# Attention and two expert layers on one core: where v_m w_in and the scores stand in TensorE's queue

## The chip, the cores and the metric

One core of a Trainium2 chip runs the whole program in one launch. The metric is the device time of an execution in microseconds (us); of several executions the median is taken.

## The reference, cut to what matters

```python
a = softmax(phi, axis=seq)                   # b=8, h=8, s=576, m=32
k_m = einsum('bhsm,bhsd->bhmd', a, k)        # d=64
v_m = einsum('bhsm,bhsd->bhmd', a, v)
attn = softmax(q @ k_m.T / 8)                # 576 x 32 for each head: P
x = (attn @ v_m) as [4608, 512]
h = x @ w_in;  g = h - tanh(h);  x2 = g @ w_out          # d_ff = 2048
h = x2 @ w_in2; g = h if h > 0 else exp(h) - 1; out = g @ w_out2
```

The weights and all matrices are float32. The kernel splits what it multiplies with into a high and a low part (the helper `convert` does it for weights, 128 rows by 512 at a time) and adds three products.

## The kernel before, in words

**Stage 1** is `moe_kernel`'s loop over 64 `blocks`. A block is one slice of 288 tokens (`n`, two slices to a batch) with two of the eight pages of 256 hidden columns (`sw` is the pair of pages). Attention times w_in is not made in that order: `make_vw` first multiplies v_m with the two pages of w_in (L337, called v_m w_in below), two blocks share the result, and `h_unit` (L355, the P product) multiplies P with it. A block has two halves, one for each page, and a half is written out by hand in this order: the P product into `h_ps`; ScalarE's first functions of it (L366 to L368); a first `x_unit` (L406, the product with w_out, of an older slice); a round of the weight conversions; a first round of the attention units, `units.round()`; in the first half of an odd block v_m w_in for the next two blocks (L808; in block 1 page by page, one in each half); a second `x_unit`; VectorE's three operations on `h_ps` (L382 to L384); a second round of the units. Below, 7.0 is the first half of block 7.

**Attention** runs beside it as 16 units, two to a batch, each a Python generator (`Attention.unit`). A round takes every live unit one step, to its next `yield`, the oldest first. Unit `u` starts in a listed round (L634). The steps of a unit from 2 on, in rounds after its start: 1 a transpose (mT), 3 the largest value (bmax), 7 the sums k_m and v_m (km, 24 products), 9, 10, 12 and 13 transposes of q (pq), 11 that of k_m and v_m (kT_ps, after which v_m is there), 14 the scores (sc), 19 the split of P, 21 its store to DRAM. Between 3 and 4 and between 7 and 8 (`spaced`) a bank of PSUM is kept over the `yield`. Before the blocks, rounds are run until unit 1 has stored its P (L635); from the seventh on, each of them also takes a round of the conversions (`cv`).

**PSUM.** x, v_m w_in (two banks), the scores (two banks) and every other product of the units share the three banks of `misc`; the P product has four banks of its own and the conversions have one.

**Conversions.** `cv` is a queue: every second round starts one conversion of half a page, those in `first` ahead of those in `todo`. A conversion takes four operations of VectorE (L50, L51, L54, L57) and one of ScalarE (L48); all but those of the first layer's w_in take another of ScalarE (L62) and one of GpSimd (L64). The half pages of w_out pages 0 and 1 stand in `todo`; at block 0 pages 2 and 3 of w_in and w_out go into `first` (L770). `need` runs rounds of `cv` until a page is there, in block 1 with rounds of the units beside them (L560). When the last unit has stored its P, page 7 of w_out goes into `first` (L775); at blocks 26 and 30 pages 4 to 7 of w_in go in ahead of what is there.

Each engine takes its instructions in the order in which this Python code issues them; so does the DMA queue of SyncE, on which all loads and stores go. The order of the rounds therefore is the order of TensorE's, VectorE's and ScalarE's queues.

Stage 2 (layer 2, L466 and L508) begins at about 880 us and is not touched.

## Time and profile before

| | |
|---|---|
| median of 3 runs | 1699.24 us |
| lowest and highest | 1696.74 and 1699.35 us |
| the profiled execution, its own time | 1696.12 us |
| span of its trace, first to last instruction | 1694.1 us |
| mean granted TensorE clock | 0.975 of full speed |

The span is 2.0 us shorter than the time of the same execution; the rest lies around it. The profile lists, for each engine, when it was busy, and for each idle stretch what released the engine. PE is TensorE, PEld its weight loads, DVE VectorE, ACT ScalarE, POOL GpSimd.

### The profile page before, as it was taken

How to read it: one execution, taken by the hardware profiler on the slowest of the kernel's cores; microseconds unless marked ns; L12 is line 12 of the kernel's file. 1: busy time of each engine (PE TensorE's matmuls, PEld its weight loads, DVE VectorE, ACT ScalarE, POOL GpSimd, SP SyncE). 2: the span in 40 equal slices, each digit the busy share in tenths (PEclk: the TensorE clock that was granted, in tenths of full speed). 3: DMA queues.
4: the chain of work that ended last, by engine and by line, in shares of the span. 5: the costliest groups of instructions: out<-in, count | busy, mean ns of one | idle time of the engine just before them, and what ended most of it. 6: DMA issues, size and time to landing. Idle time of an engine off the chain costs nothing.

```text
span 1694.1 us, 28080 instructions
## 1 busy us (share of the span) xinstructions
PE 1589.7 (94%) x10742; PEld 1382.9 (82%) x10742; DVE 1146.7 (68%) x1680; ACT 896.6 (53%) x1623; POOL 745.2 (44%) x526
## 2 busy tenths in 40 slices
PE   6639899889999989999999999999999999999998
PEld 4528788778889989999999988888888888888886
DVE  6766667878888878888675655655565555565554
ACT  2436767767787768888763333333333333333332
POOL 1325556666675557777662322232232232232222
PEclk9769999999999999999999999999999999999999
DMA  9635766668565446666579321212121212121100
GB/s 235 191 117 160 203 192 207 206 203 251 191 229 175 163 149 217 214 221 206 169 254 351 105 63 50 64 49 74 39 75 50 63 50 75 50 70 55 29 9 25
DMA packets 142214, 232.90 MB, mean 137 GB/s; under 512 B 8704, under 2 KB 102912, under 8 KB 140032
## 3 DMA queue, kind: packets, MB, share of 16 engines
q1 hardware_dynamic: 142080, 231.11, 42.8%
q8 instruction: 84, 1.38, 0.3%
q14 instruction: 50, 0.41, 0.1%
HBM read 157.68 MB, written 73.40 MB: 136 GB/s over the span
## 4 chain that ended last, share of the span: by engine, by line
PE 60%; POOL 5%; DVE 4%; ACT 3%; issue 3%; DMA 1%; POOLq 0%; ACTq 0%; DVEq 0%
PE h_ps L466 24%; PE o_ps L508 23%; PE x_ps L406 9%; PE h_ps L355 4%; POOL g L391 2%; POOL v L373 2%; DVE s L383 1%; POOL wst L64 1%; DVE s L384 1%; DVE h_ps L382 1%; DMA x_dram<-x 1%; ACT t L366 1%; ACT x L412 1%; ACT big L377 1%; ACT g L390 0%
## 5 line engine op out<-in xcount | busy, mean ns | idle before, releaser
L406 PE MATMUL x_ps<-g,w 128*128 128x288 f32 x3072 | 448.6, 298 | 45.8 <-ACT w L62 25.8
L406 PEld LDWEIGHTS x_ps<-g,w 128*128 128x128 f32 x3072 | 420.3, 190 | 64.0 <-ACT w L62 26.3
L492 POOL TENSOR_TENSOR e<-hm,e 128x512 fp32r<-128x512 f32 x144 | 186.7, 1297 | 573.0 <-ACT e L491 525.6
L466 PE MATMUL h_ps<-x,wi 128*128 128x512 f32 (+1 forms) x1920 | 422.2, 370 | 0.0
L508 PE MATMUL o_ps<-wo,e 128*128 128x512 f32 x1728 | 420.3, 392 | 0.7 <-POOL e L492 0.7
L466 PEld LDWEIGHTS h_ps<-x,wi 128*128 128x128 f32 x1920 | 336.0, 188 | 65.7
L508 PEld LDWEIGHTS o_ps<-wo,e 128*128 128x128 f32 x1728 | 323.6, 188 | 72.4 <-POOL e L492 1.1
L477 ACT ACTIVATE t_ps<-hm 128x512 f32<-128x512 f32 x144 | 86.7, 602 | 500.7 <-DVE hm L476 500.7
L373 POOL TENSOR_TENSOR v<-t,u 128x576 f32<-128x576 f32 x128 | 183.9, 1437 | 183.5 <-ACT u L367 157.5
L391 POOL TENSOR_TENSOR g<-s,g 128x576 fp32r<-128x576 f32 x128 | 201.5, 1574 | 90.0 <-ACT g L390 86.0
L483 DVE SCALAR_TENSOR_TENSOR hm<-hm,t_ps 128x512 f32<-128x512 f32 x144 | 98.9, 687 | 200.3 <-ACT hm L478 200.3
L355 PE MATMUL h_ps<-p,vw 128*128 128x288 f32 x1536 | 233.4, 302 | 0.0
L355 PEld LDWEIGHTS h_ps<-p,vw 128*128 128x128 f32 x1536 | 214.8, 192 | 2.9 <-issue 2.4
L476 DVE TENSOR_SCALAR hm<-h_ps 128x512 f32<-128x512 f32 x144 | 99.5, 691 | 125.9 <-PE h_ps L466 123.2
L366 ACT ACTIVATE t<-h_ps 128x576 f32<-128x576 f32 x128 | 83.3, 650 | 131.0 <-PE h_ps L355 56.5
L383 DVE SCALAR_TENSOR_TENSOR s<-s,v 128x576 f32<-128x576 f32 x128 | 137.5, 1074 | 12.5 <-POOL v L373 12.5
L368 ACT ACTIVATE s<-u,bias 128x576 f32<-128x576 f32 x128 | 99.5, 777 | 33.2 <-POOL g L391 25.4
L384 DVE COPY_PREDICATED s<-big,h_ps 128x576 f32<-128x576 uint32 x128 | 106.7, 834 | 11.0
L382 DVE TENSOR_TENSOR h_ps<-h_ps,t 128x576 f32<-128x576 f32 x128 | 96.7, 755 | 13.4 <-ACT u L367 13.4
L485 DVE TENSOR_TENSOR hm<-hm,h_ps 128x512 f32<-128x512 f32 x144 | 98.9, 687 | 5.0
L484 DVE SCALAR_TENSOR_TENSOR hm<-hm,t_ps 128x512 f32<-128x512 f32 x144 | 98.9, 687 | 5.0
L377 ACT ACTIVATE big<-u,bias 128x576 f32<-128x576 f32 x128 | 98.0, 766 | 1.1 <-DVE s L384 0.9
(88 smaller groups left out, 1552.4 us busy)
## 6 DMA issues: line engine op xcount, KB each, us to landing
x_dram<-x SPq DMA_DIRECT2D x128, 288.0 KB, 3.0
xr<-x_dram SPq DMA_DIRECT2D x72, 512.0 KB, 3.8
p<-p_dram SPq DMA_DIRECT2D x62, 576.0 KB, 5.0
raw<-in_moe_w_in_dram SPq DMA_DIRECT2D x32, 512.0 KB, 4.5
raw<-in_moe_w_out_dram SPq DMA_DIRECT2D x32, 512.0 KB, 4.0
w_dram<-wst SPq DMA_DIRECT2D x32, 512.0 KB, 3.6
kv<-in_k_dram SPq DMA_DIRECT2D x16, 576.0 KB, 6.0
kv<-in_v_dram SPq DMA_DIRECT2D x16, 576.0 KB, 7.9
```

The source lines that it names most:

```text
L355: nc.tensor.matmul(ps[:, j, :NB], lhsT=vw[a][:, kc, c0 + 128 * j:c0 + 128 * j + 128], rhs=p[:, kc, b, :], start=(k == 0), stop=(k == 5))
L366: nc.scalar.activation(t, w[0], ACTF.Tanh)
L373: nc.gpsimd.tensor_tensor(v, t, u, op=ALU.mult)
L377: self.nc.scalar.activation(big, u, ACTF.Relu, bias=self.const["bias"][:, 1:2])
L382: nc.vector.tensor_tensor(d, d, t, op=ALU.subtract)
L383: nc.vector.scalar_tensor_tensor(s, s, G_B, v, op0=ALU.add, op1=ALU.mult)
L384: nc.vector.copy_predicated(s, big.bitcast(U32), d)
L391: nc.gpsimd.tensor_tensor(g[:, 1], s, r32(g[:, 0]), op=ALU.subtract)
L406: nc.tensor.matmul(ps, lhsT=wo[pg][a][:, j, 128 * dm:128 * dm + 128], rhs=self.g[n, pg][:, b, j, :], start=(k == 0), stop=(k == 11))
L466: nc.tensor.matmul(out, lhsT=w3[:, a, kc, 128 * j:128 * j + 128], rhs=x[:, b, kc, :], start=(i == 0), stop=(i == 11))
L492: nc.gpsimd.tensor_tensor(e[:, 1], hm, r32(e[:, 0]), op=ALU.subtract)
L508: nc.tensor.matmul(acc, lhsT=e[:, a, jj, 128 * tg:128 * tg + 128], rhs=w4[:, b, j, :], start=(k == 0 and jj == 0 and i == 0), stop=(k == l ...
```

## The change

Three things change. (1) v_m w_in of both pages (from block 3 on) is issued at the start of the second half of an odd block, ahead of its P product, if no unit keeps a bank over a `yield` just then (`held`); otherwise it is issued in the middle of the second half. (2) The scores of units 5 to 15 wait, step by step, until the round is one that a P product follows (the second of a half) and no bank is kept. A flag `busy` lets only one unit at a time be between its first transpose of q and its scores. (3) Every unit has one more empty step ahead of its scores.

```diff
--- before.py
+++ after.py
@@ -89,6 +89,7 @@
         self.q_p = pool("at_q", 2)
         self.phi_p = pool("at_phi", 2 if side == "left" else 1)
         self.loaded = {}
+        self.before_x, self.held, self.busy = False, 0, False
         fix = pool("at_fix", 1)
         self.n_t = 3 if side == "left" else 2
         self.kv = fix.tile([96, self.n_t, 4, 6, D], F32, name="kv")
@@ -151,7 +152,9 @@
         bmax = busy_tile(4 * M, "bmax")[:96].rearrange("p (h m) -> p h m", h=4)
         nc.tensor.matmul(bmax, lhsT=self.ones[:, :96], rhs=dmax, start=True, stop=True)
         if spaced:
+            self.held += 1
             yield
+            self.held -= 1
         bm = row("bm")[:96]
         nc.scalar.activation(bm, bmax, ACTF.Copy)
         av = a.rearrange("p c h m -> p h c m")
@@ -173,7 +176,9 @@
             nc.tensor.matmul(km[:, 2 * D:2 * D + 2], lhsT=a[:, c].rearrange("p h m -> p (h m)"), rhs=self.ones[:96, :2],
                              start=(c == 0), stop=(c == 5))
         if spaced:
+            self.held += 1
             yield
+            self.held -= 1
         rs = sm.tile([128, 1], F32, tag="rs", name="rs")
         nc.vector.tensor_scalar(rs, km[:, 2 * D:2 * D + 1], GUARD, None, op0=ALU.add)
         nc.vector.reciprocal(rs, rs)
@@ -182,6 +187,9 @@
         nc.vector.tensor_scalar(kvs, twice, rs, None, op0=ALU.mult)
         yield
         self.load(nxt, "kv")
+        while self.busy:
+            yield
+        self.busy = True
         qT = wk.tile([128, 4, 3, 96], F32, tag="qT", name="qT")
         for pr in range(2):
             qt = self.loaded.pop((u, f"q{pr}"))
@@ -203,6 +211,9 @@
                 nc.scalar.activation(self.vm_dst(b)[r].rearrange("p h m -> p (h m)"), kT_ps[r, 1, :], ACTF.Copy)
                 self.vm_done.add(u)
                 yield
+        yield
+        while u > 4 and (self.before_x or self.held):
+            yield
         s = self.sc_p.tile([128, 18, M], F32, tag="s", name="s")
         sc = [ps_tile([128, 512], "sc") for _ in range(2)]
         keep_busy(nc, ident, sc[0][:, 384:], beside.get(("sc", u), 0))
@@ -211,6 +222,7 @@
                 r = slice(64 * cp, 64 * cp + 64)
                 nc.tensor.matmul(sc[cp][32 * h:32 * h + 32, :NB], lhsT=kT[r, h, :],
                                  rhs=qT[r, h].rearrange("p c q -> p (c q)"), start=True, stop=True)
+        self.busy = False
         for cp in range(2):
             nc.vector.transpose(s[:, 9 * cp:9 * cp + 9].rearrange("p j m -> p (j m)"), sc[cp][:, :NB])
         yield
@@ -645,6 +657,17 @@
         def make_vw(b, pgs):
 
             m1.vw_unit(vm[:, b // 2], {pg: wi[pg][0] for pg in pgs}, b, pgs)
+
+        def vw_soon(b, sw, half=None):
+
+            pgs = [2 * sw, 2 * sw + 1] if half is None else [2 * sw + half]
+            for pg in pgs:
+                need("i", pg, half is not None)
+            while not all(u in vm_done for u in range(2 * b + 2)):
+                units.round()
+            if half != 1:
+                m1.new_vw(b, sw, bi // 2 % 2 ^ 1)
+            make_vw(b, pgs)
 
         m1.new_vw(0, 0, 0)
         for pg in range(2):
@@ -785,6 +808,9 @@
             p_there |= p_done
             for i in range(2):
                 pg = 2 * sw + i
+                if vw_next and bi > 1 and i == 1 and not at1.held:
+                    vw_soon(*vw_next)
+                    vw_next = None
                 m1.h_unit(sw, n, pg)
                 if (bi, i) == (0, 0):
                     cv.round()
@@ -802,19 +828,13 @@
                 m1.g_big(n, pg)
                 if (bi, i) != (0, 0):
                     cv.round()
+                at1.before_x = True
                 units.round()
+                at1.before_x = False
                 if pend:
                     m1.g_d(*pend.pop())
-                if vw_next and (bi == 1 or i == 0):
-                    vb, vsw = vw_next
-                    pgs = [2 * vsw + i] if bi == 1 else [2 * vsw, 2 * vsw + 1]
-                    for vpg in pgs:
-                        need("i", vpg, bi == 1)
-                    while not all(u in vm_done for u in range(2 * vb + 2)):
-                        units.round()
-                    if i == 0:
-                        m1.new_vw(vb, vsw, bi // 2 % 2 ^ 1)
-                    make_vw(vb, pgs)
+                if vw_next and (bi == 1 or i == 1):
+                    vw_soon(*vw_next, i if bi == 1 else None)
                 if soon and bi > 60:
                     soon.popleft()()
                 x_next(bi < 22)
```

## Rows read from the trace of the kernel before

**Rows 1.** The page: busy us of each engine, its share of the span, instructions.

```profile
PE 1589.7 (94%) x10742; PEld 1382.9 (82%) x10742; DVE 1146.7 (68%) x1680; ACT 896.6 (53%) x1623; POOL 745.2 (44%) x526
```

**Rows 2.** Six stretches: their us, busy us of PE, PEld, DVE, ACT, POOL, clock, DMA.

```profile
40.00:59.55 19.55, 14.29 (x111) 10.76 (x104) 14.90 (x33) 5.25 (x14) 3.03 (x2) 0.59 0.64 195
59.55:84.00 24.45, 16.23 (x157) 12.08 (x156) 19.80 (x31) 15.35 (x30) 11.26 (x8) 0.85 0.61 170
84.00:111.00 27.00, 2.79 (x14) 2.30 (x10) 21.31 (x33) 7.76 (x14) 6.32 (x6) 0.50 0.40 130
111.00:158.00 47.00, 42.42 (x425) 37.13 (x426) 28.84 (x47) 26.35 (x52) 23.12 (x16) 0.93 0.52 152
158.00:480.80 322.80, 292.62 (x2787) 259.04 (x2786) 242.78 (x376) 234.11 (x463) 202.80 (x145) 0.98 0.66 203
480.80:600.80 120.00, 118.19 (x1023) 112.79 (x1022) 104.32 (x150) 95.67 (x168) 74.15 (x52) 1.00 0.55 190
```

**Rows 3.** TensorE in time: start, us, line, tiles, count, [idle before <-releaser].

```profile
110.88 0.61 PE L406 MATMUL x_ps<-g,w 128*128 128x288 f32 x1 [24.21 <-ACT w L62]
```

**Rows 4.** VectorE in time: first and fourth operation of a conversion, the next first.

```profile
85.50 0.70 DVE L50 TENSOR_SCALAR cv_m<-cv_m 128x512 f32<-128x512 f32 x1
...
87.70 0.69 DVE L57 SCALAR_TENSOR_TENSOR w<-raw,cv_m 128x512 uint32<-128x512 uint32 x1
89.07 0.70 DVE L50 TENSOR_SCALAR cv_m<-cv_m 128x512 f32<-128x512 f32 x1 [0.69 <-ACT cv_m L48]
```

**Rows 5.** VectorE and GpSimd: one line all 128 times, and two groups of the page.

```profile
L383 DVE SCALAR_TENSOR_TENSOR s<-s,v x128: 735/758/4546, 64.3 to 881.7; 128x576 f32<-128x576 f32 x128
...
L373 POOL TENSOR_TENSOR v<-t,u 128x576 f32<-128x576 f32 x128 | 183.9, 1437 | 183.5 <-ACT u L367 157.5
...
L383 DVE SCALAR_TENSOR_TENSOR s<-s,v 128x576 f32<-128x576 f32 x128 | 137.5, 1074 | 12.5 <-POOL v L373 12.5
```

**Rows 6.** TensorE, groups, 158 to 481 us: busy us, mean ns, idle before, releasers.

```profile
L406 PE MATMUL x_ps<-g,w 128*128 128x288 f32 x1068 | 159.4, 300 | 10.9 <-ACT x L412 4.8 <-DVE vw L342 4.4 <-ACT qT L193 0.9
...
L170 PE MATMUL km<-kv,a 96*32 96x192 f32 x480 | 23.5, 348 | 8.2 <-ACT x L412 3.4 <-ACT a L163 3.4 <-ACT g L390 1.3
...
L337 PE MATMUL vw_ps<-w,vm 64*32 64x256 f32 x352 | 17.1, 383 | 5.3 <-ACT x L412 2.8 <-ACT qT L193 1.3 <-ACT vm L203 0.9
...
L143 PE MATMUL mT<-ident,cmax 96*128 96x96 f32 x9 | 2.5, 277 | 1.4 <-DVE s L215 1.2 <-ACT x L412 0.2
```

**Rows 7.** TensorE in time, block 7, its v_m w_in and what follows.

```profile
207.04 0.62 PE L337 MATMUL vw_ps<-w,vm 64*32 64x256 f32 x2 [0.36 <-ACT x L412]
208.57 1.09 PE L337 MATMUL vw_ps<-w,vm 64*32 64x256 f32 x30 [0.92 <-ACT qT L193]
211.12 3.25 PE L406 MATMUL x_ps<-g,w 128*128 128x288 f32 x12 [1.45 <-DVE vw L342]
...
214.55 2.92 PE L355 MATMUL h_ps<-p,vw 128*128 128x288 f32 x12
```

**Rows 8.** TensorE in time, a half block without attention.

```profile
476.07 1.74 PE L355 MATMUL h_ps<-p,vw 128*128 128x288 f32 x12
477.65 3.33 PE L406 MATMUL x_ps<-g,w 128*128 128x288 f32 x24
```

**Rows 9.** TensorE in time, halves 37.1 and 38.0.

```profile
606.83 0.40 PE L406 MATMUL x_ps<-g,w 128*128 128x288 f32 x1 [1.54 <-ACT w L62]
610.11 0.85 PE L406 MATMUL x_ps<-g,w 128*128 128x288 f32 x2 [2.88 <-POOL w L64]
610.76 3.08 PE L355 MATMUL h_ps<-p,vw 128*128 128x288 f32 x12
613.64 4.54 PE L406 MATMUL x_ps<-g,w 128*128 128x288 f32 x24
```

**Rows 10.** Waits of TensorE, 481 to 860 us: total us, times, longest us.

```profile
PE x_ps L406 <- ACT x L412: 2.4, 8, 0.5
PE vw_ps L337 <- DVE w L57: 1.6, 2, 0.8
```

## The prediction

> **What bounds the kernel now.** I read the busy shares first: TensorE is busy for 94% of the span [rows 1], so a change of order can only give back stretches in which its queue stands. Busy times by stretch show where [rows 2]. From 480.8 to 600.8 us TensorE is busy for 118.2 of 120 us; little is to be had there. From 158 to 480.8 us, with the attention units beside the blocks, it is busy for 292.6 of 322.8 us, and the weight loads, whose ends are not modelled, say more: 259.0 us, where the share of the quiet stretch (112.8 of 120) would need 275.6; that is 47 us too many. From 59.55 us, where the first P product starts, to 158 us, where w_out pages 2 and 3 are first used, TensorE works for 61.4 of 98.5 us. One wait makes most of that: the first x stands 24.2 us for one conversion (the high part, L62) at the granted clock of 0.50 [rows 2, 3].
>
> **Why that wait is there, and what the empty step does to it.** One conversion starts every second round, in the order of the queue. By the code, unit 1 stores its P in round 17 (counted from 0); the prologue then ends after 12 rounds of conversions, which have started all but one of the queue's entries: the second half of w_out page 1 is left. At block 0 twelve conversions go in ahead of it, and the thirteenth round starts one of those. So the first x must run 16 rounds of `need`. The empty step (3) makes unit 1 store in round 18. The prologue has 13 rounds of conversions, and the thirteenth now starts the missing half page. By my count no round of `need` for w_out is then left ahead of the first x; instead `need` runs three rounds (two before) for w_in page 2, two (none) for page 3, and two (none) for w_out page 3 in block 3. The first five of these step the units too. With the prologue's extra round the units stand four rounds, one block, further ahead of the blocks than now.
>
> **A. The start, −11 us.** The conversions are moved, not removed. One takes four operations of VectorE of 0.70 us, and back to back one begins every 3.57 us [rows 4]: six of them now lie under the 24 us and must go beside blocks 1 to 3. VectorE worked for 19.8 + 21.3 + 28.8 = 70.0 us from 59.55 to 158 us [rows 2] and must do so again ahead of the same x. In the stretch where it already sets the pace it was busy for 19.8 of 24.45 us, 81% [rows 2]. At that share 70.0 us take 86.4 us, not 98.5: 12.1 us are won. Against it, unit 1's last steps stand behind half a conversion more (1.4 us) while VectorE is busy for 14.9 of 19.55 us, and ahead of v_m w_in stands another half (1.4 us), which block 0 no longer has to do; I charge 1 us net. Bounds: VectorE at 100% gives 28 us, no better pace than now 0, and a prologue later by both halves with nothing won +3 us.
>
> What speaks against A: L383 reads two tiles in SBUF. Its median is 0.758 us, its mean 1.074 and its longest 4.546 us, and GpSimd's L373 beside it takes 1.437 us [rows 5]. The Trainium skill, SBUF — State Buffer, "Who interferes with whom", says that such a VectorE instruction and a GpSimd one that reads SBUF exclude each other for a whole instruction, and by it the sum's A would be rival 1's; the trace agrees as far as L383's spread goes. For the sum I keep 81%, since the stretch that it is from holds L383 and GpSimd's work too.
>
> **B. Blocks 4 to 25, −16 us.** TensorE's rows [rows 6] have 5.3 us of waiting ahead of v_m w_in (L337), and behind it x waits 4.4 us for VectorE's part of it, 0.9 us for q's copy, and 2.1 us for a bank at block 25 (part of the 4.8 us for x's own copies; I give it that value from the longest of these). Block 7 also loses clock: after three waits, x takes 3.25 us and the P product 2.92 us, where a quiet half has 1.67 and 1.74 us [rows 7, 8]: 2.8 us. Together 15.5 us for eleven v_m w_in. Ahead of a P product, which needs no `misc` bank, the two banks have 1.7 us of TensorE's work in which to be emptied, and x takes the third. What is late next: three of the eleven (blocks 13, 19, 21) come right behind scores and the next unit's first transpose of q, and must wait for VectorE to empty the scores' banks; two (9, 15) find a bank kept and go to the middle of the half as now. Five at about 1.3 us leave 6.5 us, so 9 us are won. On ScalarE and VectorE the evacuation moves by half a half block and costs the same.
>
> The scores: now km waits 3.4 us for x's copy and mT 1.2 us for the scores' transposes [rows 6], both in the scores' round. Held to the second round these end. But `busy` lets the next unit's waiting transpose of q go in the same round, between scores and P product; by my count 9 of 11 scores have it. It needs x's bank, so it waits for ScalarE's copy. No row shows this; the nearest are v_m w_in's waits for two copies of ScalarE, 0.36 and 0.92 us [rows 7]. Between 0 and 0.92 us each I take 0.4, by the first, which is x's copy too: 3.6 us. 1 us is won. P comes later by up to five rounds in a unit, but the units are four rounds ahead of the blocks; by my count every P still loads half a block or more before its use, so I cost its stores, loads and queue at nothing. If the head start were missing, P for blocks 18 and 26 would be loaded right before use.
>
> These 10 us are idle by modelled ends, of 30 us in all; the weight loads show 47, so I scale to 13. The four rounds of unit work that moved into A (one km, a tenth of 23.5 us [rows 6], and some transposes) leave 3 us less here. Sum 16. Bounds: nothing of it (a loss is rival 4), or all of 15.5 and 4.6 scaled and the 3, 33.
>
> **C. Halves 37.1 and 38.0, −7 us.** x waits 1.54 and 2.88 us for the second half of w_out page 7, and the next P product and two x run at the lower clock, 3.08 and 4.54 against 1.74 and 3.33 us [rows 8, 9]: 7.0 us. The units now end in block 24, not 25, so page 7 enters `first` a block earlier and its first half starts ahead of w_in pages 4 to 7; the second then has its last step at the start of 37.0 and not in the x that waits. Bounds 0 and 7.
>
> **D. Blocks 27 to 61, −4 us.** x and v_m w_in wait 2.4 + 1.6 us there [rows 10]; a P product between covers both. Bounds 0 and 6 (by the same 1.5).
>
> **Sum.** 11 + 16 + 7 + 4 = 38 us off the profiled execution's 1696.1 us: 1658 us. The median before is 3.1 us above that execution; I leave the forecast at 1658 us for the median too. Stage 2 is not touched. A measurement of this kernel tells about 0.2% (3.4 us) from no change.
>
> **Rivals.**
> 1. *VectorE only just carries the start.* If each of the eight L383 of blocks 0 to 3 stands for a whole instruction of GpSimd, 1.44 us [rows 5], VectorE needs 11.5 us more: A is 0, the rest holds: 1669 us. For it: 70 us of work in a shorter stretch, and L383's mean above its median. Against: between 111 and 158 us VectorE was busy for 28.8 of 47 us only. Chance 0.18.
> 2. *The order is not what I counted*: the missing half page is still behind the twelve. A and C are 0 and the units have no head start, which takes 3 from B: P is late for blocks 18 and 26, at block 7's price of 6 us (below) each. 1696 − 13 − 4 + 12 = 1691 us. Chance 0.05.
> 3. *TensorE stays at the lower clock through blocks 0 to 3*, as it did from 84 to 111 us after standing (0.50, that is 1.2 GHz, against 1.00). Its 16.2, 2.8 and 42.4 us at 0.85, 0.50 and 0.93 are 54.7 us of work at the full clock and 109 us at half, 10.5 more than the 98.5: A is +10.5 instead of −11, 1680 us. The Trainium skill, TensorE: Matmul & The Clock Gate, "HAM oscillation", describes such falls and returns around waits. Against: from 60 to 84 us the clock was 0.85 on a TensorE busy for two thirds. Chance 0.07.
> 4. *Slower: scores, transpose and v_m w_in hold all three banks at once*, and the P product, which needs none, stands behind them in TensorE's queue. Block 7 has the price: 4.4 us from the first wait to x, less 1.1 us of work, and 2.8 us of clock, about 6 us [rows 7]. At each of the 11 scores that is 66 us; with A, C, D and the 15.5 + 4.6 us removed, 1696 − 42 + 66 = 1720 us. It decides above 42/11 = 3.8 us for each. Against: mT, which waits for scores' transposes today, loses 1.2 us in all [rows 6]. Chance 0.06.
>
> **Numbers.** The forecast has 0.64. 1658 us is its value; alone it spans 1637 to 1676 us. The range of 1637 to 1682 us takes in rivals 1 and 3 and leaves out 2, 4 and the better bounds of A and B. Faster: the forecast, rivals 1 and 3 and 0.02 of rival 2, 0.91; within 0.2%: the rest of rival 2, 0.03; slower: rival 4, 0.06.
>
> **What would show it.** Right: no wait of x for L62 near 85 us; the first use of w_out pages 2 and 3 at about 147 us; the last scores in block 22 and not 23; between 158 and 480 us no x that waits for L342, and L337 with few waits; nothing at halves 37.1 and 38.0. Wrong: a new wait of x in block 3 for w_out page 3 (L62, L64); transposes of q or v_m w_in that wait for the scores' transposes (L215) for over 1 us each; a clock below 0.9 from 60 to 150 us; a P product that waits for P.

## The result, and the profile after

The changed kernel takes 1677.37 us (median of 4 runs, 1673.64 to 1678.64), beside 1698.45 us of the kernel before on the same chip: a ratio of 0.9873, with an interval of 0.9855 to 0.9891. That is 21 us less; 38 were forecast. The profiled execution took 1677.41 us and its span is 1675.3 us, 18.8 less than before. Where the 18.8 us came from is read from the starts of the P products (`h_ps<-p,vw`) in TensorE's timeline; here and in the table further down a stretch is the distance between two of them:

| us | before | after | forecast |
|---|---|---|---|
| start of 0.0 | 59.55 | 63.45 | (in A) |
| 0.0 to 4.0 | 100.6 | 94.9 | A, with the start: -11 |
| 4.0 to 26.0 | 320.7 | 309.7 | B: -16 |
| 26.0 to 37.1 | 120.0 | 117.6 | D, with the last but one: -4 |
| 37.1 to 38.1 | 17.2 | 10.1 | C: -7 |
| 38.1 to 63.0 | 251.8 | 255.4 | D |
| the rest | 824.3 | 824.2 | 0 |

Thus A gave 1.8 us and not 11, B 11.0 and not 16, C 7.1 as forecast, and D lost 1.2 where 4 were to be won: 2.4 up to block 36, and 3.6 lost from 38 on.

The page's busy times of the engines after the change, beside [rows 1]:

```profile
PE 1585.5 (95%) x10742; PEld 1381.5 (82%) x10742; DVE 1201.6 (72%) x1680; ACT 900.9 (54%) x1623; POOL 737.5 (44%) x526
```

The same number of instructions, but VectorE is busy for 55 us more. One line has most of it (L395, which was L383), in the same two groups as in [rows 5]:

```profile
L385 POOL TENSOR_TENSOR v<-t,u 128x576 f32<-128x576 f32 x128 | 183.5, 1434 | 177.2 <-ACT u L379 129.2 <-DVE s L396 14.3 <-DVE vw L354 13.9
...
L395 DVE SCALAR_TENSOR_TENSOR s<-s,v 128x576 f32<-128x576 f32 x128 | 183.7, 1435 | 15.2 <-POOL v L385 15.2
```

Its mean went from 1074 to 1435 ns: 46 us. The stretches after the change, as in [rows 2] (the prologue's end, from the first P product to the first x, from there to block 4, blocks 4 to 25, the quiet ones):

```profile
40.00:63.45 23.45, 15.24 (x130) 11.72 (x122) 20.13 (x41) 6.69 (x19) 3.03 (x2) 0.65 0.71 224
63.45:98.54 35.09, 22.03 (x211) 16.15 (x210) 23.01 (x39) 17.12 (x33) 13.79 (x10) 0.74 0.52 150
98.54:158.30 59.76, 49.88 (x453) 42.83 (x453) 49.76 (x75) 34.77 (x69) 30.22 (x22) 0.91 0.55 157
158.30:468.04 309.74, 280.78 (x2715) 251.96 (x2712) 249.86 (x370) 230.81 (x453) 204.39 (x143) 0.99 0.68 211
468.04:588.04 120.00, 119.54 (x1040) 115.11 (x1039) 114.97 (x152) 96.93 (x169) 73.39 (x51) 1.00 0.54 182
```

The stretch of 27 us at a clock of 0.50 [rows 2] is gone, and with it the wait of [rows 3]; the first x, in TensorE's timeline, waits for something else, and briefly:

```profile
98.54 1.81 PE L418 MATMUL x_ps<-g,w 128*128 128x288 f32 x6 [0.97 <-DVE vw L354]
```

Halves 37.1 and 38.0 [rows 9] now take 5.35 and 4.80 us, with one wait of 0.17 us, behind v_m w_in:

```profile
585.63 1.89 PE L367 MATMUL h_ps<-p,vw 128*128 128x288 f32 x12
587.36 1.75 PE L418 MATMUL x_ps<-g,w 128*128 128x288 f32 x12
589.28 1.87 PE L418 MATMUL x_ps<-g,w 128*128 128x288 f32 x12 [0.17 <-DVE vw L354]
590.98 1.77 PE L367 MATMUL h_ps<-p,vw 128*128 128x288 f32 x12
592.59 3.36 PE L418 MATMUL x_ps<-g,w 128*128 128x288 f32 x24
595.78 1.77 PE L367 MATMUL h_ps<-p,vw 128*128 128x288 f32 x12
```

### The profile page after: what moved, and what is told of

Read it like the earlier page. It is cut to its first block, busy times and chain, and to the rows that moved or that the text cites. A ratio compares the mean times of both kernels' runs of the same rounds, so it can differ in the third digit from the quotient of the medians.

```text
span 1675.3 us, 28135 instructions
## 1 busy us (share of the span) xinstructions
PE 1585.5 (95%) x10742; PEld 1381.5 (82%) x10742; DVE 1201.6 (72%) x1680; ACT 900.9 (54%) x1623; POOL 737.5 (44%) x526
## 4 chain that ended last, share of the span: by engine, by line
PE 63%; DVE 9%; issue 2%; POOL 2%; ACT 1%; DMA 0%; DVEq 0%; SPq 0%; POOLq 0%; ACTq 0%
PE h_ps L478 24%; PE o_ps L520 24%; PE x_ps L418 10%; PE h_ps L367 4%; DVE s L395 3%; DVE s L396 2%; DVE h_ps L394 1%; DVE x L426 1%; POOL g L403 1%; POOL v L385 1%; PE vw_ps L349 1%; DVE vw L354 0%; DVE cv_m L50 0%; ACT big L389 0%; DMA p<-p_dram 0%
## 5 line engine op out<-in xcount | busy, mean ns | idle before, releaser
L418 PE MATMUL x_ps<-g,w 128*128 128x288 f32 x3072 | 441.7, 297 | 10.7 <-DVE vw L354 5.4
L403 POOL TENSOR_TENSOR g<-s,g 128x576 fp32r<-128x576 f32 x128 | 192.4, 1503 | 85.8 <-ACT g L402 77.3
L367 PEld LDWEIGHTS h_ps<-p,vw 128*128 128x128 f32 x1536 | 214.1, 192 | 13.7 <-issue 12.4
L395 DVE SCALAR_TENSOR_TENSOR s<-s,v 128x576 f32<-128x576 f32 x128 | 183.7, 1435 | 15.2 <-POOL v L385 15.2
L396 DVE COPY_PREDICATED s<-big,h_ps 128x576 f32<-128x576 uint32 x128 | 106.8, 834 | 13.6 <-ACT t L378 0.5
```

Of the source, the lines that this page charges most:

```text
L367: nc.tensor.matmul(ps[:, j, :NB], lhsT=vw[a][:, kc, c0 + 128 * j:c0 + 128 * j + 128], rhs=p[:, kc, b, :], start=(k == 0), stop=(k == 5))
L395: nc.vector.scalar_tensor_tensor(s, s, G_B, v, op0=ALU.add, op1=ALU.mult)
L396: nc.vector.copy_predicated(s, big.bitcast(U32), d)
L403: nc.gpsimd.tensor_tensor(g[:, 1], s, r32(g[:, 0]), op=ALU.subtract)
L418: nc.tensor.matmul(ps, lhsT=wo[pg][a][:, j, 128 * dm:128 * dm + 128], rhs=self.g[n, pg][:, b, j, :], start=(k == 0), stop=(k == 11))
```

## The experiments

Twelve kernels in three groups, each group beside the kernel before on one chip. "Ratio" is to that. The stretches are those of the first table, of one profile each; "s<-s,v" is the mean of L383 (L395) in ns, over all 128 and over those from 600 to 880 us.

| | us | ratio [interval] | 0.0 at | 4.0 at | 4.0-26.0 | 26.0-37.1 | 37.1-38.1 | 38.1-63.0 | s<-s,v, from 600 |
|---|---|---|---|---|---|---|---|---|---|
| before | 1698.45 | 1 | 59.6 | 160.1 | 320.7 | 120.0 | 17.2 | 251.8 | 1074, 990 |
| after | 1677.37 | 0.9873 [0.9855, 0.9891] | 63.4 | 158.3 | 309.7 | 117.6 | 10.1 | 255.4 | 1435, 1615 |
| 1 empty step | 1677.14 | 0.9891 [0.9876, 0.9906] | 64.9 | 157.0 | 315.0 | 119.8 | 9.6 | 249.5 | 1079, 1132 |
| 2 v_m w_in | 1689.57 | 0.9963 [0.9951, 0.9976] | 61.7 | 161.7 | 314.9 | 117.7 | 16.3 | 254.7 | 1358, 1401 |
| 3 v_m w_in, hold | 1697.83 | 1.0011 [1.0, 1.0021] | 60.8 | 160.6 | 323.3 | 118.9 | 16.6 | 254.4 | 1338, 1431 |
| 4 cv round | 1678.89 | 0.9906 [0.9889, 0.9924] | 63.7 | 155.1 | 317.2 | 119.7 | 9.6 | 249.5 | 1156, 1133 |
| 5 late old | 1672.9 | 0.9864 [0.9851, 0.9877] | 65.9 | 158.1 | 310.0 | 119.7 | 9.6 | 249.5 | 1145, 1130 |
| 6 no hold | 1682.49 | 0.9927 [0.9914, 0.994] | 63.0 | 159.0 | 314.1 | 117.9 | 10.1 | 255.1 | 1451, 1623 |
| 7 launch | 1677.55 | 0.9893 [0.988, 0.9906] | 59.8 | 154.8 | 316.8 | 119.8 | 9.5 | 249.5 | 1147, 1132 |
| 8 launch, v_m w_in | 1678.13 | 0.9896 [0.9883, 0.9908] | 60.6 | 151.6 | 321.9 | 119.7 | 9.6 | 249.5 | 1192, 1122 |
| 9 launch, both | 1674.37 | 0.9865 [0.9849, 0.9881] | 63.6 | 154.7 | 318.1 | 117.9 | 9.5 | 249.6 | 1184, 1081 |
| 10 low on VectorE | 1711.89 | 1.0087 [1.0073, 1.0101] | 65.5 | 157.8 | 310.0 | 117.6 | 10.1 | 283.6 | 1053, 745 |
| 11 hold, empty | 1672.95 | 0.9856 [0.9839, 0.9872] | 64.9 | 158.3 | 309.2 | 119.8 | 9.5 | 249.5 | 1101, 1132 |
| 12 after again | 1675.27 | 0.9876 [0.9858, 0.9894] | 62.4 | 154.5 | 310.2 | 117.6 | 10.1 | 255.3 | 1404, 1613 |

### Which of the parts does it?

**1. The kernel before, with the empty step alone.**

```diff
+        yield
         s = self.sc_p.tile([128, 18, M], F32, tag="s", name="s")
```

> The kernel before with one more empty step ahead of every unit's scores, and nothing else of the change. Theory 1 (the empty step works through the conversions: it lets the thirteenth round start the second half of w_out page 1 before block 0): the first x no longer waits 24 us, halves 37.1 and 38.0 lose their 7 us of waiting as in the changed kernel, the first P product starts about 4 us later, and the units stand a block ahead: 7 + 2 + 2 us off, about 1687 us against 1698. Theory 2 (the gain comes from where v_m w_in and the scores stand; the empty step only spaces the scores from the transposes of q): no difference, 1698 us, and the 24 us wait stays.

1677.14 us, 10 less than I had expected: the empty step alone gives nearly what the whole change gives (0.9891 beside 0.9873). What of the start the other parts add or take is within the scatter of one profile (below).

**2. The kernel before, with v_m w_in moved as in the change, and nothing held, no empty step.** Against the changed kernel:

```diff
-        while self.busy:
-            yield
-        self.busy = True
...
-        yield
-        while u > 4 and (self.before_x or self.held):
-            yield
...
-        self.busy = False
```

> The kernel before with v_m w_in ahead of the P product alone (no held scores, no empty step). Theory 1: the conversions stay as before, so the 24 us wait and the wait at half 37.1 stay; blocks 4 to 25 lose most of the 13 us that v_m w_in costs them there, 8 us, and the late blocks change by under 3 us either way: about 1690 us. Theory 2: nearly the whole of the 21 us, about 1680 us. Third (VectorE and GpSimd get in each other's way when v_m w_in is moved): the duration of the operation s<-s,v rises as in the changed kernel (mean 1.44 against 1.07 us) and the late blocks get slower by 3 us or more, about 1693 us.

1689.57 us: 6 us less in blocks 4 to 25, 3 us more from block 38 on, where s<-s,v is longer. C stays: without the head start halves 37.1 and 38.0 wait as before (16.3 us).

**3. The changed kernel without the empty step.**

```diff
-        yield
         while u > 4 and (self.before_x or self.held):
```

> The changed kernel without the empty step. Theory 1: the 24 us wait and that at half 37.1 are back, and the units lose the block that they were ahead, so P for blocks 18 and 26 is loaded right before use and the P product waits about 3 us at each; blocks 4 to 25 otherwise win 8 to 11 us as in the changed kernel: 1692 us, between 1688 and 1699. Theory 2: 1677 us as the changed kernel.

1697.83 us: no gain is left. Held scores without the head start cost 8 us in blocks 4 to 25 beside run 2. A part of it is P, which is late for block 26 (TensorE's waits, 460 to 490 us), as I had said of a missing head start:

```profile
PE h_ps L366 <- DMA p<-p_dram: 3.7, 1, 3.7
```

**4. The kernel before, with one round of the conversions more, and no step of the units.**

```diff
             if units.rounds >= 7:
                 cv.round()
+        cv.half()
+        cv.round()
```

> The kernel before with one more round of conversions behind the prologue's loop, and nothing else: by the code the order of conversions and the number of need rounds are then those of the changed kernel, while no step of a unit is delayed. Theory 1: as the empty step alone or a little better, since unit 1's last steps do not stand behind another half conversion: 1684 to 1688 us, no 24 us wait, no wait at half 37.1, the units a block ahead. Theory 2: 1698 us. A third (the prologue's delay of 4 us in the changed kernel comes from the conversion itself, not from the unit's extra round): the first P product starts at 63 us here too.

1678.89 us, 5 less than the range that I had given. So the empty step works through the conversion that it lets start; the units' extra step is not needed for A and C. The first P product comes at 63.7 us here too: the round's own operations, on VectorE ahead of v_m w_in's copy, are what delays it.

### What do the others cost?

**5. The changed kernel, v_m w_in from block 26 on in its old place.**

```diff
-                if vw_next and (bi == 1 or i == 1):
+                if vw_next and (bi == 1 or i == 1 or bi > 25):
                     vw_soon(*vw_next, i if bi == 1 else None)
+                    if bi > 25:
+                        vw_next = None
```

> The changed kernel with v_m w_in of the blocks from 26 on back in the middle of the first half, as in the kernel before. My theory (the move shifts VectorE's s<-s,v against GpSimd's operation so that one stands for the other, and this costs more in blocks 38 to 62 than the removed waits give): the mean of s<-s,v over 600 to 880 us falls from 1.6 us to 1.1 us or less, the stretch from block 38 to 62 is 4 to 6 us shorter, blocks 26 to 36 1 to 2 us longer; 1671 to 1674 us. Rival (the place of v_m w_in has nothing to do with it, blocks 38 to 62 are slower because of the clock or of what the earlier end of the units leaves): 1677 us, and the late mean of s<-s,v stays at 1.5 us or more.

As my theory had it: the late mean of s<-s,v falls from 1615 to 1130 ns, blocks 38 to 62 take 249.5 us, 5.9 less, blocks 26 to 36 2.1 us more. How the two engines stand to each other is seen in the timeline, VectorE and GpSimd of the changed kernel first:

```profile
675.37 0.76 DVE L394 TENSOR_TENSOR h_ps<-h_ps,t 128x576 f32<-128x576 f32 x1
675.42 1.43 POOL L403 TENSOR_TENSOR g<-s,g 128x576 fp32r<-128x576 f32 x1 [1.50 <-ACT g L402]
676.03 1.43 DVE L395 SCALAR_TENSOR_TENSOR s<-s,v 128x576 f32<-128x576 f32 x1
...
680.59 1.42 POOL L403 TENSOR_TENSOR g<-s,g 128x576 fp32r<-128x576 f32 x1
680.83 1.80 DVE L395 SCALAR_TENSOR_TENSOR s<-s,v 128x576 f32<-128x576 f32 x1
```

and the same operations in this run:

```profile
664.52 0.75 DVE L395 SCALAR_TENSOR_TENSOR s<-s,v 128x576 f32<-128x576 f32 x1
664.99 1.58 POOL L403 TENSOR_TENSOR g<-s,g 128x576 fp32r<-128x576 f32 x1 [1.56 <-ACT g L402]
...
671.67 0.75 DVE L395 SCALAR_TENSOR_TENSOR s<-s,v 128x576 f32<-128x576 f32 x1
```

Where GpSimd's L403 begins first, L395 ends 0.61 and 0.62 us behind its end, whenever it began (676.03 + 1.43 against 675.42 + 1.43), and so do all 49 of this kind from 600 to 880 us; where L395 begins first it takes 0.75 us, and it is GpSimd that is longer (1.58 for 1.43). The Trainium skill, SBUF — State Buffer, "Who interferes with whom", states that a VectorE instruction with two SBUF inputs contends with a GpSimd instruction that reads SBUF, and that the order of issue decides which of them blocks; these rows agree with it.

**6. The changed kernel without the held scores and without `busy`.**

```diff
-        while self.busy:
-            yield
-        self.busy = True
...
-        while u > 4 and (self.before_x or self.held):
-            yield
...
-        self.busy = False
```

> The changed kernel without the held scores and without the flag that lets one unit at a time between its transposes of q and its scores: v_m w_in moved, and the empty step. Theory (with the units a block ahead the hold costs as much on TensorE as it removes, and what counts is v_m w_in's move): blocks 4 to 25 as in the changed kernel within 2 us, 1675 to 1679 us. Rival (the hold removes waits of km and mT worth some 4 us): 1681 us or more. Second rival (the hold itself costs, because the transposes of q then stand between scores and P product): 1671 to 1674 us.

My theory fell, the rival holds: 1682.49 us, blocks 4 to 25 take 4.4 us more. The hold is worth something; run 11 shows the most of where.

**7. The kernel before, with the missing conversion started ahead of block 0, without a round of the others.**

```diff
+        soon_o = cv.todo.popleft()
+        next(soon_o)
+        cv.live.append(soon_o)
+        cv.wait = 2
```

> The kernel before, with nothing but the missing conversion (second half of w_out page 1) started ahead of block 0, without a round in which the other conversions move too. Theory (what the gain of the empty step consists of is that this conversion starts ahead of the twelve of block 0; the 4 us by which the first P product comes later are the other conversions' operations, moved ahead of it in VectorE's queue): the x that waited 24 us does not wait, the first P product starts at 60 to 61 us and not at 63 to 65 us, blocks 4 to 63 as in the run with one round of conversions; 1673 to 1676 us. Rival (the 4 us only move: the work has to be done ahead of the same x, and block 0 is then longer by as much): 1677 to 1680 us.

The first P product came at 59.8 us, 3.9 earlier than in run 4, as I had said, but block 4 at 154.8 and not 151: the rival is right, the 4 us only move. In TensorE's timeline the lead over run 4 is 1.6 us at the first x (93.13 against 94.73 us) and gone at the first x that uses w_out page 2 (152.50 against 152.10 us).

**8. That start, with v_m w_in ahead of the P product below block 26; no scores held, no empty step.**

```diff
-                if vw_next and (bi == 1 or i == 0):
+                if vw_next and (bi == 1 or i == 1 or bi > 25):
```

(and the change's `vw_soon` ahead of the P product, `held` counted, as in the change)

> The start of the run before (missing conversion started ahead of block 0, no empty step), and v_m w_in ahead of the P product in blocks below 26 only, in its old place from there on; no scores held. Theory (the parts add: the start as there, 5 us less in blocks 4 to 25 from v_m w_in, nothing lost in blocks 38 to 62): 1667 to 1671 us. Rival (v_m w_in's move is worth nothing once the units run a block ahead, because the waits for banks only change places): 1673 to 1676 us, as the run with the conversion alone.

Missed: 1678.13 us, above the rival's range too, which had the parts not add. Block 4 begins 3.2 us earlier than in run 7, and blocks 4 to 25 take 5.1 us more.

### The exclusion alone, the hold alone, the parts together

**9. Launch in place of the empty step, the hold, v_m w_in ahead up to block 35.**

```diff
-        yield
         while u > 4 and (self.before_x or self.held):
...
-                if vw_next and bi > 1 and i == 1 and not at1.held:
+                if vw_next and 1 < bi < 37 and i == 1 and not at1.held:
```

(with the lines of run 7, and run 5's condition with 36 for 25)

> The parts that paid, together: the missing conversion started ahead of block 0 in place of the empty step, the scores held, v_m w_in ahead of the P product in blocks 3 to 35 only and in its old place from block 37 on. Theory (they add: the h of block 4 begins at 152 to 155 us, blocks 4 to 25 take 310 to 312 us as in the changed kernel, blocks 38 to 62 take 249.5 us as before): 1666 to 1671 us, faster than the changed kernel by 6 to 11 us. Rival (without the empty step the units' steps fall on other halves, v_m w_in finds a bank kept more often, and the start's 3 us come back in blocks 4 to 25, as they did when v_m w_in was moved without the hold): 1672 to 1676 us.

The rival: 1674.37 us. The late blocks are as hoped (117.9 and 249.6 us), the start too, but blocks 4 to 25 take 318.1 us, 8.4 more than with the empty step. One wait of v_m w_in for the scores' transposes is 3.0 us here, for 1.5 at most in the changed kernel (TensorE's waits of 150 to 475 us):

```profile
PE vw_ps L348 <- DVE s L226: 4.8, 3, 3.0
```

In sum, though, TensorE waits ahead of its groups no longer than there, 29.3 us for 29.0. It is busy for longer, 288.8 us for 280.8: the lower clock (1.2 of 2.4 GHz) was granted for 17.1 us of the stretch, there for 6.8; one km more stands in it (480 products for 436, 1.8 us); and the P products run at 320 ns a product for 305 (TensorE's groups, 154.7 to 472.8 us, clock 0.97, then 158.3 to 468.0 us, clock 0.99):

```profile
L366 PE MATMUL h_ps<-p,vw 128*128 128x288 f32 x528 | 87.9, 320 | 0.0
```
```profile
L367 PE MATMUL h_ps<-p,vw 128*128 128x288 f32 x528 | 82.2, 305 | 0.0
```

**10. The changed kernel, the low part of g made by VectorE from block 38 on.**

```diff
-        nc.gpsimd.tensor_tensor(g[:, 1], s, r32(g[:, 0]), op=ALU.subtract)
+        self.low.tensor_tensor(g[:, 1], s, r32(g[:, 0]), op=ALU.subtract)
...
+            m1.low = nc.vector if bi > 37 else nc.gpsimd
```

> The changed kernel with GpSimd's second operation of each half (the low part of g, g<-s,g) done by VectorE from block 38 on; the arithmetic is the same. Theory (s<-s,v is long in the late blocks because it stands for that operation on GpSimd and for nothing else): the mean of s<-s,v over 600 to 880 us falls from 1.62 us to 0.8 to 1.0 us, though VectorE has 50 operations more; its busy time there stays about as it was, and blocks 38 to 62 take 249 to 256 us; 1672 to 1678 us. Rival (it is long for another reason, as its operand in PSUM or a transfer): its mean stays at 1.4 us or more, VectorE has some 40 us more to do, and the time is 1680 us or more.

Half right. VectorE's groups of 600 to 880 us:

```profile
L403 DVE TENSOR_TENSOR g<-s,g 128x576 fp32r<-128x576 f32 x48 | 41.2, 858 | 48.4 <-ACT g L402 48.4
...
L395 DVE SCALAR_TENSOR_TENSOR s<-s,v 128x576 f32<-128x576 f32 x48 | 35.7, 745 | 0.0
```

With L403 gone from GpSimd, s<-s,v takes 745 ns and no more, with v_m w_in in its new place: it stood for that operation (in this window of the changed kernel 49 of its 51 begin while L403 runs). But the time was missed, 1711.89 us: VectorE's queue now stands 48.4 us for ScalarE's high part of g, 1 us in each half, which I had not counted.

**11. The changed kernel with v_m w_in in its old place throughout.**

```diff
-                if vw_next and bi > 1 and i == 1 and not at1.held:
-                    vw_soon(*vw_next)
-                    vw_next = None
...
-                if vw_next and (bi == 1 or i == 1):
+                if vw_next and (bi == 1 or i == 0):
```

> The changed kernel with v_m w_in in its old place throughout: the held scores and the empty step remain. Theory (the hold pays for itself, since the next unit's sums and v_m w_in no longer meet the scores' banks): blocks 4 to 25 take 310 to 313 us, blocks 38 to 62 take 249.5 us; 1671 to 1674 us, no slower than the changed kernel. Rival (the hold pays only with v_m w_in out of the way, and this out of the way only with the hold): blocks 4 to 25 take 314 to 317 us; 1676 to 1679 us.

As the theory had it: 1672.95 us, 309.2 us in blocks 4 to 25. So between these blocks v_m w_in's move gave nothing to a kernel with the other two parts. TensorE's two groups in this run, and in the changed kernel, both over blocks 4 to 25:

```profile
L418 PE MATMUL x_ps<-g,w 128*128 128x288 f32 x1056 | 157.4, 300 | 11.0 <-DVE vw L354 4.9 <-ACT x L424 4.7 <-POOL g L403 1.5
...
L349 PE MATMUL vw_ps<-w,vm 64*32 64x256 f32 x352 | 14.3, 382 | 0.4
```
```profile
L418 PE MATMUL x_ps<-g,w 128*128 128x288 f32 x1056 | 154.8, 298 | 3.6 <-ACT x L424 2.0 <-POOL g L403 1.3 <-ACT bm L159 0.3
...
L349 PE MATMUL vw_ps<-w,vm 64*32 64x256 f32 x352 | 15.5, 402 | 8.4 <-DVE kvs L187 4.0 <-DVE s L227 3.3 <-ACT x L424 1.0
```

The move takes 7.4 us of waiting from x and gives 8.0 to v_m w_in itself, which at its new place comes right behind km or the scores and waits until VectorE has read their banks.

Run 1 loses 5.8 us to run 11 in these blocks, and the largest loss at one place is as much, at halves 18.1 and 19.0; the other halves differ by up to 3.2 us either way and cancel. The P products of 18.1 and 19.1 stand 23.0 us apart in run 1 (369.50 and 392.49) and 17.2 in run 11. TensorE and ScalarE in run 1, then in run 11:

```profile
374.01 0.78 ACT L369 ACTIVATE s<-u,bias 128x576 f32<-128x576 f32 x1 [1.36 <-POOL g L392]
...
376.16 0.67 ACT L236 ACTIVATE phl<-phl 128x576 fp32r<-128x576 f32 x1
...
377.03 0.83 ACT L163 ACTIVATE a<-a 96x768 f32<-96x768 f32 x1
...
377.92 4.07 PE L170 MATMUL km<-kv,a 96*32 96x192 f32 x48 [3.10 <-ACT a L163]
381.91 2.71 PE L356 MATMUL h_ps<-p,vw 128*128 128x288 f32 x12
```
```profile
379.12 2.16 PE L173 MATMUL km<-kv,a 96*32 96x192 f32 x48 [1.22 <-ACT a L166]
381.21 1.86 PE L367 MATMUL h_ps<-p,vw 128*128 128x288 f32 x12
```

In run 1 an older unit's steps fall in the same rounds: ScalarE waits 1.36 us for GpSimd, which is late by that unit's operations, and then has the split of its P (L236) to do ahead of the exponential `a` that km needs. Km waits 3.10 us, for 1.22 in run 11, and km and the P product behind it run in part at the lower clock (0.85 over these 23 us, 1.00 in run 11). The hold has moved that unit's steps to other rounds. Run 6, without the hold, loses there too: its two halves take 22.8 us and the changed kernel's 17.7. So the hold pays, but not by what it was counted for. (The flag `busy` goes with it in every run; what the flag does alone was not tried.)

**12. The changed kernel again.**

> The changed kernel once more, beside the three others on one chip, so that they can be compared with it directly: 1675 to 1679 us, blocks 4 to 25 in 309 to 311 us, blocks 38 to 62 in 255 to 256 us. A first P product at another time than 63.4 us, with the h of block 4 again at 158 us, would say that the end of the prologue does not set the start.

1675.27 us. Its first P product came at 62.4 and block 4 at 154.5 us, the changed kernel's at 63.4 and 158.3, though the two are one code; runs 5 and 10, the same code up to block 25, have 158.1 and 157.8. The stretch from 0.0 to 4.0 took 92.1, 92.2 and 92.3 us in runs 12, 5 and 10 and 94.9 in the first profile. VectorE and GpSimd there, of the first profile and of this:

```profile
138.76 1.83 POOL L161 TENSOR_TENSOR a<-phi,bm 96x768 f32<-96x768 f32 x1 [0.39 <-ACT bm L159]
139.20 3.39 DVE L395 SCALAR_TENSOR_TENSOR s<-s,v 128x576 f32<-128x576 f32 x1
140.54 1.42 POOL L403 TENSOR_TENSOR g<-s,g 128x576 fp32r<-128x576 f32 x1
```
```profile
138.20 1.41 DVE L395 SCALAR_TENSOR_TENSOR s<-s,v 128x576 f32<-128x576 f32 x1
```

In the first, L395 began 0.44 us behind GpSimd's L161 and was done 0.63 us behind the end of the L403 that followed it: two operations of GpSimd, back to back, kept it for 3.39 us. Behind it TensorE waits for v_m w_in's evacuation and then runs the 52 products of its filler (L70, below) in 7.49 us at a clock of 0.80, for 6.00 us in run 12.

Of the kernels tried, run 11 has the lowest ratio, 0.9856, but its interval and the changed kernel's beside it (0.9876) overlap; the medians on that chip are 2.3 us apart. That it is better rests on the stretches: 5.9 us less from 38.1 on and 2.2 us more from 26.0 to 37.1, the same in runs 5 and 11.

## Why the prediction was right, and where not

The direction, the order and the range held: 1677.37 us lies within 1637 to 1682, 19 us above the forecast of 1658. It lies there by the range's upper end, which stood for rivals 1 and 3; what came short is A, B and D, and D for a reason that no rival had. The counts of rounds held: the x that waited no longer does, the last scores are in block 22, the wait of [rows 9] is gone.

**A, forecast 11, measured 1.8 us** (2.0 to 5.6 in the three other profiles of the code, 12, 5 and 10). By the prediction's own mark, the first use of w_out pages 2 and 3, it is 3.6 us: that x starts at 154.45 us, where 147 was forecast and the kernel before has 158.03. Behind it a km of the units' head start (2.16 us) now stands ahead of block 4's P product. TensorE before, then after:

```profile
152.28 6.00 PE L70 MATMUL x_ps<-ident 128*128 128x128 f32 x52
158.03 1.85 PE L406 MATMUL x_ps<-g,w 128*128 128x288 f32 x12
```
```profile
147.21 7.49 PE L70 MATMUL x_ps<-ident 128*128 128x128 f32 x52
154.45 1.83 PE L418 MATMUL x_ps<-g,w 128*128 128x288 f32 x12
156.22 2.16 PE L173 MATMUL km<-kv,a 96*32 96x192 f32 x48
```

L70 is a filler that the kernel puts ahead of this x (`keep_busy`, not touched). TensorE is there 5.1 us earlier than before; in this profile the filler takes 1.5 us longer, as run 12 shows.

That the wait ends was right (runs 1 and 4), the size of the gain was not. Two terms of the step failed. The prologue's delay was charged at 1 us net; it is 3.9 us, since the whole round of conversions stands ahead of v_m w_in's copy. And VectorE at 81% of 70.0 us of work was to reach that x in 86.4 us; it took 91.0 us, and 94.9 to 4.0, since it was busy for 23.01 + 49.76 = 72.8 us of these, 77%. The share came from a stretch where VectorE set the pace, and the later one had not been such: GpSimd was done with the last of w_out page 3 (L64) at 112.6 us before, 45 us ahead of the x that uses it, and at 152.98 us after, 1.5 us ahead. Of the 2.8 us more work a part is s<-s,v, as run 12 shows. VectorE's own waits from 63.4 to 158.3 us are these:

```profile
DVE cv_m L50 <- ACT cv_m L48: 8.5, 4, 5.1
DVE h_ps L394 <- ACT u L379: 3.4, 1, 3.4
DVE vw L354 <- ACT vw L353: 3.2, 2, 1.6
```

The longest of the first kind, in the timeline of VectorE and ScalarE:

```profile
84.34 0.65 ACT L378 ACTIVATE t<-h_ps 128x576 f32<-128x576 f32 x1 [3.17 <-PE h_ps L367]
...
89.53 0.61 ACT L48 ACTIVATE cv_m<-raw 128x512 f32<-128x512 f32 x1
90.17 0.41 ACT L201 ACTIVATE qT<-pq 128x288 f32<-128x288 f32 x1
90.17 0.70 DVE L50 TENSOR_SCALAR cv_m<-cv_m 128x512 f32<-128x512 f32 x1 [5.10 <-ACT cv_m L48]
```

ScalarE waits for the P product, then does eleven operations, of the block, the units and an earlier conversion, and only then L48, the first operation of the next conversion. A conversion that runs beside blocks hangs on ScalarE's queue, and through it on TensorE; before, six of them ran under the first x's wait, where ScalarE was busy for 7.8 of 27 us only [rows 2, 3]. Rival 1 (VectorE only just carries the start, A is 0, 1669 us) was the nearer story for A, in part by its own mechanism; rival 3 had a part in it, with the clock at 0.74 up to the first x, above the 0.5 that it assumed. Its sign, a clock below 0.9 from 60 to 150 us, is there (0.82), but the kernel before has 0.77.

**B, forecast 16, measured 11.0 us; the parts were wrong.** It was worked out from waits that would end, of 30 us ahead of TensorE's groups before, and scaled from 10 to 13 by weight loads that show 47; 47/30 would make it 15.7, so 13 was a choice and no sum. By the groups of blocks 4 to 25 the sum of the idle times ahead of them is 29.0 us after the change (x 3.6, v_m w_in 8.4, km 4.5, bmax 5.7, q 3.6, mT 2.4, scores 0.8) and 27.7 in run 11: waits change places, nothing more. The 9 us of v_m w_in are 0 (run 11 against the changed kernel) and the 1 us of the held scores is 5.8 (run 11 against 1). The step that failed is "what is late next": I put five v_m w_in, three behind scores and two in the middle of the half, at 1.3 us each, and took the rest as free; the trace has 8.4 us ahead of v_m w_in, 4.0 of them for VectorE's reading of km (L187), which I had not counted, and 3.3 for the scores. What fell is the time that TensorE is busy, from 290.5 us (160.1 to 480.8 us) to 280.8. By its groups, whose times overlap, km has 3.7 us of it, 2.2 of them the one km of the units' head start (forecast with the other moved work at 3), x 2.8, the scores 2.2, v_m w_in 1.6 and the transposes of q 1.1. The clock has a part in it: the lower level was granted for 13.7 us of the stretch before and for 6.8 after; at half speed that makes some 3.4 us, an estimate. That B came to two thirds of its forecast is luck: what it was added up from did not happen.

The parts do not add. Moving v_m w_in changed blocks 4 to 25 by -5.8 us (run 2), -0.9 (6 against 1), +0.5 (after against 11) and +5.1 (8 against 7), the hold by -5.8 (11 against 1), -4.4 (after against 6) and +8.4 (3 against 2). Where a part costs 5 us or more, the lower clock has a share in it: it was granted for 20.5 us of these blocks in run 8 and 13.7 in run 3, and for 6.8 in runs 1, 2, 6, 7 and 11 and in the changed kernel.

**C, forecast 7, measured 7.1 us.** Right in mechanism and size. Runs 1, 4 and 7 have it with the missing conversion alone; runs 2 and 3 lack it with all the rest.

**D, forecast 4 won, 1.2 us lost.** The part up to block 36 was right: 2.2 us of its 2.4 are v_m w_in's move (117.6 against run 11's 119.8). From block 38 on the move costs 5.9 us (255.4 against 249.5). The waits of [rows 10] did not need it: in run 11, with v_m w_in in its old place, x waits 0.4 us from 38.1 to 63.0, and the stretch is 2.3 us shorter than before. What the step left out: with v_m w_in's evacuation at another place, VectorE reaches s<-s,v mostly just behind the start of GpSimd's g<-s,g, stands for it, and is late with the next v_m w_in, for which x then waits. TensorE's group from 600 to 880 us, of the changed kernel, then of run 11:

```profile
L418 PE MATMUL x_ps<-g,w 128*128 128x288 f32 x1290 | 182.7, 296 | 4.3 <-DVE vw L354 3.8 <-POOL g L403 0.5
```
```profile
L418 PE MATMUL x_ps<-g,w 128*128 128x288 f32 x1298 | 184.3, 296 | 1.2 <-POOL g L403 0.9
```

These 3.8 us are the larger part of the 5.9. In the timeline L395 takes 1.63 us from 649.01 on, L396 and L354 follow it on VectorE, and x at 652.19 has waited 0.37 us for L354; no run takes the exclusion away and leaves the rest, so that its price is read from there and not measured alone. The P product now comes right behind v_m w_in and takes 1.2 us more from 38.1 to 63.0 (87.4 against 86.2), and its weight loads stand 4.9 us there, 12 times 0.4, for nothing that the profile shows; they do so in run 10 too, where the exclusion is gone.

VectorE is busy for 250.2 of the 280 us from 600 on, against 222.2 before and 227.0 in run 11. What failed in D is thus the overlap, which was put at no cost: the exclusion was in the prediction as a price for the start alone.

**The rivals.** 2 did not come (the order was as counted). 4 did not come: v_m w_in waits for the scores' transposes three times, 0.9, 0.9 and 1.5 us; one of these is over the 1 us that was named as a sign, and its 3.8 us were never reached.

## What to carry to other kernels

In an order woven by hand, a wait that a row shows is not a wait that goes away: sum the idle time ahead of all of an engine's groups before and after, and TensorE's time at the lower clock with it, and look at what the moved step will stand behind at its new place. A change that moves an evacuation by half a block also moves VectorE against GpSimd; before it is made, look which of the two starts first where a VectorE operation reads two tiles in SBUF and a GpSimd one runs beside it, as L395 and L403 do here, since the later one can pay up to a whole operation, in every block. And take the parts of a change apart one by one, and then in pairs: here one empty `yield` was nearly the whole gain, and a part that was worth 6 us alone cost 5 in another order.

## What the runs showed that I had not expected

One s<-s,v took 3.39 us, kept by two operations of GpSimd that came one behind the other (1.83 and 1.42 us), without a turn between them. That is not so each time. In the kernel before, L383 begins at 676.73 us and ends 0.61 us behind GpSimd's L64, after 0.92 us, though L391 follows L64 directly; there it is L391 that is longer, 1.97 us. What decides stays open. And one code does not have one time in its start: block 4 began at 154.5, 157.8, 158.1 and 158.3 us in four profiles, of which the stretch with that operation explains 2.7 us (94.9 against 92.2, with the filler behind it) and the start of the first P product, 62.4 to 65.9 us, the rest; why that start varies stays open. A single profile is not enough to size a term of 2 us there, though the later stretches repeat within 0.5 us.
